# Softmax sums turned by block transposes on VectorE instead of products on TensorE, in an attention and convolution kernel

## The chip, the core and the metric

The kernel runs on one core of a Trainium2 chip. The metric is the device time of one execution in microseconds (us); the median of three runs stands for the kernel. PE is TensorE, DVE VectorE, ACT ScalarE, POOL GpSimd, and SP the engine that issues most DMAs. "PEld" is the part of PE that loads weights.

## The reference

Two independent results are put side by side: `a`, a long convolution over 2048 positions of 448 channels (an S4D state-space layer), and `b`, full softmax attention with 16 heads of width 28. The change touches `b` alone:

```python
q, k, v = qkv[0], qkv[1], qkv[2]
scale = Dh ** -0.5
scores = jnp.einsum("bhqd,bhkd->bhqk", q, k) * scale
p = _softmax(scores, axis=-1)
o = jnp.einsum("bhqk,bhkd->bhqd", p, v)
return o.transpose(0, 2, 1, 3).reshape(B, S, D) @ wo
...
return jnp.concatenate([a, b], axis=-1)
```

## The kernel before

A first phase (about 0 to 230 us) projects `q`, `k` and `v` and prepares tables for the convolution; there a scheduler orders the instructions. From then on every engine executes its instructions in the order in which the program wrote them (`nc.kept = KEPT["a"]`), each engine strictly in its own order.

The second phase is one loop of 256 steps (`for s in range(NS)`). The 16 heads are 4 groups of 4, the 2048 queries 4 stretches of 512, so there are 16 **units**, numbered 0 to 15; each has 16 steps, one for each 128 keys. A step's order is written in `ORDER`:

- `m0` to `m3` (`max_mm`) are products for a later unit's row maxima. Each takes a PSUM tile from a ring of three, `pm0`, `pm1`, `pm2` (`w_tile`). The tile of `m0` is read by ACT (`rl`), that of `m1` by DVE (an instruction that the trace calls CUSTOM_DVE_ANT_0 and the order ISA), those of `m2` and `m3` by DVE (`TENSOR_REDUCE mx<-pm`).
- `s0` to `s3` (`s_mm`) are this step's scores (`pss`), which ACT turns to `p` by an exponential.
- `pv` (`pv_step`) adds the product of the previous step's `p` with `v` to the PSUM tile `po`.
- `f` (`slot`), two of them, one ahead of `pv` and one behind it, run one waiting job each, from several queues in a fixed order of rank. A job's PSUM tile comes from the same ring of three. Jobs are parts of the convolution (`ua,w` and `ua,mt`; `e,g` and `w,ko`; later `yk,mw`, `p,mw`, `zi,wb`), the transpose `ident,m` of the maxima, and output projections (`ua,og` and `ua,on`).
- `v` (`vec`), three of them, run DVE's next part of the convolution's powers (`g`, `zg`); `k` sends POOL its parts (`e`, `eu`), products and sums of tiles in SBUF, 9 instructions for each of 56 blocks. These go on until about 985 us.

So on PE, from one `po` to the next, a step reads: job, `m2 s2 m3 s3 m0 s0 m1 s1`, job, `po`. From step 192 on (unit 12) the ring of three becomes one name with four buffers.

`fin` closes a unit, called right after its last `pv`. `po` holds 4 heads in 4 strips of 32 partitions: 28 rows of output, and in row 28 the sum of the exponentials, because the columns of `v` carry a 1 there. ACT copies `po` to `o` (128 x 512, SBUF). Then two jobs follow in slots, 2 and 4 slots later (`soon_slot(UG[1], sums)` and `soon_slot(UG[2], scale)`): `sums` multiplies `o` with the selector `sel` on PE (in 4 strips and 4 column blocks, which gives the sums with queries on partitions), DVE takes the reciprocals `r`, and ACT spreads each over 32 columns (`rb`); `scale` turns `rb` back on PE by products with the identity `ident`, and DVE multiplies `o` with that PSUM tile to `on`. For units 0 to 11 `on` goes to DRAM, for units 12 to 15 it feeds the output projections (`project`), which `scale` queues.

## Time and profile before

| | |
|---|---|
| median of 3 runs | 1278.05 us (1277.69 to 1278.42) |
| the profiled execution | 1278.83 us, of which the span from the first to the last instruction is 1277.0 us |
| granted TensorE clock | 0.982 of full speed over the span, 1.00 from 232 to 1255 us |
| busy in the span | PE 95%, ACT 76%, DVE 72%, POOL 66%, PEld 54% |

All names in the trace's rows come from the program, with buffer numbers left out; every row has line L77, that of a helper through which all instructions pass, so rows are told apart by their tiles: `po<-p,v` is a matmul that writes `po` from `p` and `v`. "x32" in a row of PE is twice the 16 matmuls of the program, because each float32 product is made in two passes that the trace shows singly. A row of the timeline has its start, its length (both in us), engine, line, operation, tiles, shapes and count; a bracket at its end is the engine's idle time just before it, and what ended that.

### The profile page before, as it was taken

How to read it: one execution, taken by the hardware profiler on the slowest of the kernel's cores; microseconds unless marked ns; L12 is line 12 of the kernel's file. 1: busy time of each engine (PE TensorE's matmuls, PEld its weight loads, DVE VectorE, ACT ScalarE, POOL GpSimd, SP SyncE). 2: the span in 40 equal slices, each digit the busy share in tenths (PEclk: the TensorE clock that was granted, in tenths of full speed). 3: DMA queues.
4: the chain of work that ended last, by engine and by line, in shares of the span. 5: the costliest groups of instructions: out<-in, count | busy, mean ns of one | idle time of the engine just before them, and what ended most of it. 6: DMA issues, size and time to landing. Idle time of an engine off the chain costs nothing.

```text
span 1277.0 us, 33251 instructions
## 1 busy us (share of the span) xinstructions
PE 1216.2 (95%) x12593; PEld 692.5 (54%) x12593; DVE 922.6 (72%) x2106; ACT 967.0 (76%) x2162; POOL 843.6 (66%) x728
## 2 busy tenths in 40 slices
PE   6788888999999999999999999999999999999998
PEld 4666764555555555555555555555555555544433
DVE  5788966877777877778778988888887645645111
ACT  5888865788888888888888888888887656656552
POOL 2666740798788888878689999989995222324321
PEclk9999898899999999999999999999999999999999
DMA  6678789436554645475533133432224533657656
GB/s 194 211 258 290 275 278 359 124 88 187 159 154 114 169 118 159 123 224 177 171 101 96 57 80 105 145 91 71 83 60 149 171 139 135 205 162 237 203 163 174
DMA packets 203528, 206.22 MB, mean 161 GB/s; under 512 B 98344, under 2 KB 162408, under 8 KB 201320
## 3 DMA queue, kind: packets, MB, share of 16 engines
q1 hardware_dynamic: 202840, 203.50, 51.8%
q8 instruction: 99, 1.62, 0.5%
q10 hardware_dynamic: 528, 0.59, 0.2%
q14 instruction: 61, 0.50, 0.1%
HBM read 121.60 MB, written 82.18 MB: 160 GB/s over the span
## 4 chain that ended last, share of the span: by engine, by line
PE 79%; DVE 9%; ACT 5%; issue 3%; POOL 2%; DMA 1%; SPq 1%; ACTq 0%; POOLq 0%; DVEq 0%
PE pm L77 44%; PE pss L77 17%; PE po L77 17%; DVE tri L77 1%; ACT tri L77 1%; DVE mx L77 1%; DVE sg L77 1%; SPq L77 1%; ACT rl L77 1%; DVE hl L77 1%; DVE px L77 1%; ACT p L77 1%; PE pt L77 1%; POOL p L77 1%; DVE g L77 1%
## 5 line engine op out<-in xcount | busy, mean ns | idle before, releaser
L77 ACT ACTIVATE p<-pss 128x512 f32<-128x512 f32 x1024 | 561.3, 611 | 111.5 <-PE pss L77 108.4
L77 PE MATMUL pss<-qhat,khat 128*128 128x512 f32 x1024 | 402.8, 399 | 1.5 <-ACT p L77 1.4
L77 DVE TENSOR_REDUCE mx<-pm 128x1 f32<-128x512 f32 x480 | 308.3, 683 | 108.9 <-PE pm L77 106.8
L77 PE MATMUL pm<-khat,qhat 128*128 128x512 f32 x749 | 326.3, 439 | 6.6 <-ACT rl L77 4.4
L77 POOL TENSOR_TENSOR e<-e,sdb 128x256 f32<-128x256 f32 x168 | 201.8, 1201 | 111.4 <-ACT e L77 62.2
L77 PE MATMUL po<-p,v 128*32 128x512 f32 x2048 | 269.1, 594 | 0.0
L77 POOL TENSOR_TENSOR e<-e,eu 128x256 f32<-128x256 f32 x168 | 248.1, 1477 | 13.2
L77 PEld LDWEIGHTS pm<-khat,qhat 128*128 128x128 f32 x749 | 141.2, 189 | 202.8 <-ACT p L77 46.9
L77 DVE CUSTOM_DVE_ANT_0 rl<-pm,rl 128x512 f32<-128x512 f32 x259 | 178.2, 688 | 73.7 <-ACT rl L77 70.8
L77 PEld LDWEIGHTS pss<-qhat,khat 128*128 128x128 f32 x1024 | 190.4, 188 | 46.1 <-issue 10.8
L77 POOL TENSOR_TENSOR eu<-e,sdb 128x256 f32<-128x256 f32 x168 | 201.9, 1202 | 0.0
L77 POOL TENSOR_TENSOR p<-pr,pr 64x448 f32<-64x448 f32 x64 | 73.1, 1142 | 161.4 <-PE pm L77 134.7
L77 ACT ACTIVATE rl<-pm 128x512 f32<-128x512 f32 x259 | 156.8, 607 | 15.4 <-PE pm L77 9.4
L77 DVE TENSOR_TENSOR g<-g,zg 128x128 f32<-128x128 f32 x392 | 161.9, 413 | 3.4
L77 PE MATMUL pm<-kdif,qhat 128*128 128x512 f32 x249 | 100.9, 405 | 6.0 <-DVE xn L77 4.1
L77 PE MATMUL pm<-xh,khat 128*128 128x512 f32 x256 | 85.0, 423 | 12.1 <-DVE hl L77 5.3
L77 DVE TENSOR_TENSOR zg<-g,zg 128x128 f32<-128x128 f32 x224 | 88.0, 393 | 5.0
L77 PEld LDWEIGHTS pm<-e,g 128*32 128x32 f32 x3584 | 57.2, 109 | 43.9 <-issue 16.2
L77 DVE TENSOR_TENSOR pr<-pm,ub 128x448 f32<-128x448 f32 x64 | 37.0, 619 | 56.4 <-PE pm L77 42.0
L77 PE MATMUL pm<-e,g 128*32 128x64 f32 x3584 | 73.0, 222 | 1.9 <-POOL e L77 1.3
L77 ACT ACTIVATE y<-pm 128x448 f32<-128x448 f32 x48 | 26.5, 553 | 58.2 <-PE pm L77 35.9
L77 ACT ACTIVATE ub<-pm 128x224 f32<-128x224 f32 (+1 forms) x96 | 38.7, 448 | 39.5 <-PE pm L77 37.4
(135 smaller groups left out, 1436.7 us busy)
## 6 DMA issues: line engine op xcount, KB each, us to landing
sdb<-sd SPq DMA_DIRECT2D x55, 336.0 KB
qhat<-q SPq DMA_DIRECT2D x64, 256.0 KB
khat<-k SPq DMA_DIRECT2D x64, 256.0 KB
sd<-sg SPq DMA_DIRECT2D x8, 1456.0 KB
k<-hl SPq DMA_DIRECT2D x16, 512.0 KB
mw<-in_mw SPq DMA_DIRECT2D x16, 512.0 KB
sd<-qhat SPq DMA_DIRECT2D x8, 896.0 KB
yu_d<-ub SPq DMA_DIRECT2D x64, 112.0 KB
```

The lines of the kernel that those rows point to most:

```text
L77: i = f(*args, **kw)
```

## The change

`sums` and `scale` leave PE. DVE turns `o` in blocks of 32 x 32 (`nc.vector.transpose`, in the order of instructions STREAM_TRANSPOSE), so that the sum of head `j` and query `32 b + i` stands on partition `32 j + i` in column 28 of block `b`; DVE takes the reciprocals of those 16 columns; ACT spreads each over the 32 columns of its block; DVE turns that back into `on`, and multiplies `o` with `on`, both now in SBUF. There are three parts, `sums`, `spread` and `scale`, and they stand in a queue of their own, `free`: they run in the next three slots after `fin` beside that slot's job, and no longer take a slot from the queues of jobs. The selector `sel`, its load in the first phase, and its constant go.

```diff
     ident = const.tile([128, 128], F32, name="ident")
     nc.sync.dma_start(ident, a["ident"])
-    sel = const.tile([128, HG], F32, name="sel")
...
         nc.sync.dma_start(kones, a["kones"])
-        nc.sync.dma_start(sel, a["sel"])
...
         on = kq_p.tile([128, CQ], F32, name="on", bufs=2)
-        rb = kq_p.tile([128, 4, HG, 32], F32, name="rb")
         og = og_u.pop(u, None)
+        t_ = {}
+        turned = lambda: kq_p.tile([128, NK, 32], F32, name="rb")
+        flat = lambda t: t.rearrange("p b e -> p (b e)")
 
         def sums():
-            pw = w_tile()
-            for t in range(4):
-                mm32(pw[:, t * HG:(t + 1) * HG], o[:, t * 128:(t + 1) * 128], sel, start=True, stop=True)
-            r = kq_p.tile([128, 4, HG], F32, name="r", bufs=2)
-            nc.vector.reciprocal(r, pw[:, :4 * HG].rearrange("p (t h) -> p t h", h=HG))
-            nc.scalar.activation(rb, r[:, :, :, None].to_broadcast([128, 4, HG, 32]), AF.Copy)
+            t = turned()
+            nc.vector.transpose(flat(t), o)
+            t_["r"] = kq_p.tile([128, NK], F32, name="r", bufs=2)
+            nc.vector.reciprocal(t_["r"], t[:, :, DH])
+
+        def spread():
+            t = turned()
+            nc.scalar.activation(t, t_["r"][:, :, None].to_broadcast([128, NK, 32]), AF.Copy)
+            nc.vector.transpose(on, flat(t))
 
         def scale():
-            pw = w_tile()
-            for t in range(4):
-                mm32(pw[:, t * 128:(t + 1) * 128], rb[:, t].rearrange("p h e -> p (h e)"), ident, True, True)
-            nc.vector.tensor_tensor(on, o, pw, ALU.mult)
+            nc.vector.tensor_tensor(on, o, on, ALU.mult)
             if g < G - 1:
                 nc.sync.dma_start(on_d[c][g], on)
...
-        soon_slot(UG[1], sums)
-        soon_slot(UG[2], scale)
+        for i, f in enumerate((sums, spread, scale)):
+            free.append((n_slot[0] + 1 + i, f))
...
     def slot(s_):
         n_slot[0] += 1
+        while free and free[0][0] <= n_slot[0]:
+            free.popleft()[1]()
         if urgent and urgent[0][0] <= n_slot[0]:
             urgent.popleft()[2]()
```

Two places of the order show what moves, both at the end of unit 7. DVE's order before; `g` and `zg` are the convolution's powers, ISA is the reader of `m1`'s tile:

```order
L77 TENSOR_TENSOR zg_10567<-g_10521,zg_10567 128x256
L77 TENSOR_REDUCE mx_10480<-pm2_10698 128x1
L77 TENSOR_REDUCE mx_10480<-pm0_10705 128x1
L77 TENSOR_TENSOR g_10521<-g_10521,zg_10567 128x16x16
L77 ISA rl_10715,mx_10480<-pm2_10721,rl_10715 128x512
L77 ISA mx_10480 128x1
L77 TENSOR_TENSOR zg_10567<-g_10521,zg_10567 128x256
L77 RECIPROCAL r_10746<-pm0_10729 128x16
L77 TENSOR_TENSOR g_10521<-g_10521,zg_10567 128x16x16
L77 TENSOR_REDUCE mx_10480<-pm2_10771 128x1
```

And DVE's order at the same place after:

```order
L77 STREAM_TRANSPOSE rb_10471<-o_10468 128x512
L77 RECIPROCAL r_10473<-rb_10471 128x16
L77 TENSOR_TENSOR zg_10348<-g_10302,zg_10348 128x256
L77 TENSOR_REDUCE mx_10261<-pm0_10482 128x1
L77 TENSOR_REDUCE mx_10261<-pm1_10489 128x1
L77 TENSOR_TENSOR g_10302<-g_10302,zg_10348 128x16x16
L77 ISA rl_10499,mx_10261<-pm0_10505,rl_10499 128x512
L77 ISA mx_10261 128x1
L77 TENSOR_TENSOR zg_10348<-g_10302,zg_10348 128x256
L77 STREAM_TRANSPOSE on_10470<-rb_10513 128x512
L77 TENSOR_TENSOR on_10470<-o_10468,on_10470 128x512
L77 TENSOR_TENSOR g_10302<-g_10302,zg_10348 128x16x16
```

Two instructions come ahead of the first pair of reduces, and two more, in place of the reciprocal, ahead of the second pair, which follows the last row; `m1` (`pm0_10505`) writes the tile that the first reduce (`pm0_10482`) has read. PE's order before, from a job in the slot ahead of the unit's last `po` to the job in the slot ahead of the next:

```order
L77 MATMUL pm_10665<-e,g 32x64 x16
L77 MATMUL po<-p,v 32x512 x4
L77 MATMUL pm_10698<-khat,qhat 128x512
L77 MATMUL pm_10705<-khat,qhat 128x512
L77 MATMUL pm_10713<-kdif_9024,qhat 128x512
L77 MATMUL pm_10721<-khat,qhat 128x512
L77 MATMUL pm_10729<-sel,o 32x4 x16
L77 MATMUL po<-p,v 32x512 x4
L77 MATMUL pm_10754<-w_111,ko 32x128 x8
```

And after (the `pss` rows between are left out in both):

```order
L77 MATMUL pm_10446<-e,g 32x64 x16
L77 MATMUL po<-p,v 32x512 x4
L77 MATMUL pm_10482<-khat,qhat 128x512
L77 MATMUL pm_10489<-khat,qhat 128x512
L77 MATMUL pm_10497<-kdif_8836,qhat 128x512
L77 MATMUL pm_10505<-khat,qhat 128x512
L77 MATMUL pm_10516<-w_110,ko 32x128 x8
L77 MATMUL po<-p,v 32x512 x4
```

The job `w,ko` moves up into the slot that `sel,o` held, and nothing stands behind the next `po`. In the first phase the scheduler also orders some instructions otherwise, by a place or a few, on all engines.

More of the change, by code (lines that the diff above doesn't have):

```diff
@@ L926, in body @@
     k_seeds(0)
-    urgent, back = collections.deque(), collections.deque()
+    urgent, free = collections.deque(), collections.deque()
     powers = {"g": collections.deque(), "e": collections.deque()}
@@ L1121, in body @@
     s = NS
-    while urgent or p_due or m_due or u_due or any(q[k] for q in (f_jobs, f_tasks, f_loaded) for k in "sf"):
+    while urgent or free or p_due or m_due or u_due or any(q[k] for q in (f_jobs, f_tasks, f_loaded) for k in "sf"):
         slot(s)
@@ L1133, in constants @@
     k["ident"] = np.eye(128)
-    sel, ones = np.zeros((128, HG)), np.zeros((128, 1))
+    ones = np.zeros((128, 1))
     for j in range(HG):
-        sel[32 * j + DH, j] = 1.0
         ones[32 * j + DH:32 * j + DH + 2] = 1.0
-    k["sel"], k["kones"] = sel, ones
+    k["kones"] = ones
     k["pw2"] = np.tile(2.0 ** np.arange(LV), (128, 1))
```

## The prediction

> **What bounds the kernel now.** First the page: busy time and the shares of the chain that ended last.

> ```profile
> PE 1216.2 (95%) x12593; PEld 692.5 (54%) x12593; DVE 922.6 (72%) x2106; ACT 967.0 (76%) x2162; POOL 843.6 (66%) x728
> PE 79%; DVE 9%; ACT 5%; issue 3%; POOL 2%; DMA 1%; SPq 1%; ACTq 0%; POOLq 0%; DVEq 0%
> ```

> PE is busy for 95% of the span and carries 79% of the chain. But a full PE says little about how much room the others have, so next comes the busy time by stage, here 700 to 800 us, in the middle of the loop.

> ```profile
> 700.00:800.00 100.00, 99.57 (x1218) 56.95 (x1218) 87.53 (x210) 84.49 (x191) 96.26 (x78) 1.00 0.28 80
> ```

> PE 99.6%, DVE 87.5%, ACT 84.5%, POOL 96.3%. PE is the bound, DVE and POOL stand right behind it. So what counts is whether DVE's new work fits at its place, not in the mean. For that I read the timeline over the end of unit 7.

> ```profile
> 733.02 1.04 PE L77 MATMUL po<-p,v 128*32 128x512 f32 x8
> 734.00 0.50 PE L77 MATMUL pm<-khat,qhat 128*128 128x512 f32 x1
> 734.16 0.60 ACT L77 ACTIVATE o<-po 128x512 f32<-128x512 f32 x1 [0.15 <-PE po L77]
> 734.27 0.43 DVE L77 TENSOR_TENSOR zg<-g,zg 128x256 f32<-128x256 f32 x1
> 734.61 1.28 DVE L77 TENSOR_REDUCE mx<-pm 128x1 f32<-128x512 f32 x2
> 735.50 0.39 PE L77 MATMUL pm<-khat,qhat 128*128 128x512 f32 x1
> 735.73 0.40 PE L77 MATMUL pss<-qhat,khat 128*128 128x512 f32 x1
> 735.81 0.41 DVE L77 TENSOR_TENSOR g<-g,zg 128x256 f32<-128x256 f32 x1
> 736.05 0.43 PE L77 MATMUL pm<-sel,o 128*32 128x4 f32 x32
> 736.33 1.06 PE L77 MATMUL po<-p,v 128*32 128x512 f32 x8
> 736.39 1.11 ACT L77 ACTIVATE p<-pss 128x512 f32<-128x512 f32 x2
> 736.55 0.69 DVE L77 CUSTOM_DVE_ANT_0 rl<-pm,rl 128x512 f32<-128x512 f32 x1 [0.33 <-PE pm L77]
> 737.76 0.50 PE L77 MATMUL pm<-khat,qhat 128*128 128x512 f32 x1
> 737.79 0.63 ACT L77 ACTIVATE rb<-r 128x512 f32<-128x512 f32 x1 [0.28 <-DVE r L77]
> 740.17 1.08 PE L77 MATMUL pm<-ident,rb 128*32 128x128 f32 x32
> 741.06 1.04 PE L77 MATMUL po<-p,v 128*32 128x512 f32 x8
> ```

> Matmuls overlap in the trace, so PE's prices are differences of starts: `m2` comes at 734.00, `m1` 1.50 us later. DVE's first reduce ends near 735.27, only 0.2 us ahead of `m1`, which needs that tile (ring of three). How hard that link is shows where an earlier product already costs DVE time, at the transpose of the maxima:

> ```profile
> 723.48 0.48 PE L77 MATMUL pm<-khat,qhat 128*128 128x512 f32 x1
> 724.07 0.28 DVE L77 SCALAR_TENSOR_TENSOR mh<-pm,mh 16x128 fp32r<-16x128 f32 x1
> 724.61 1.27 DVE L77 TENSOR_REDUCE mx<-pm 128x1 f32<-128x512 f32 x2
> 725.34 0.50 PE L77 MATMUL pm<-khat,qhat 128*128 128x512 f32 x1 [0.17 <-DVE mx L77]
> ```

> Two DVE instructions of 0.28 us push the reduces back, and `m1` starts 1.86 us after `m2` in place of 1.50: 0.36 us lost on PE. So DVE's delay there reaches PE one for one, less a margin of about 0.2.

> **What is removed.** `sel,o` holds PE from 736.05 to 736.33, 0.28 us; `ident,rb` from 740.17 to 741.06, 0.89: 1.17 together. The whole of the two groups bounds it from above:

> ```profile
> L77 PE MATMUL pm<-ident,rb 128*32 128x128 f32 x512 | 17.3, 275 | 0.6 <-ACT rb L77 0.6
> L77 PE MATMUL pm<-sel,o 128*32 128x4 f32 x512 | 7.0, 175 | 0.3 <-ACT o L77 0.3
> L77 DVE TENSOR_TENSOR on<-o,pm 128x512 f32<-128x512 f32 x16 | 10.9, 682 | 2.3 <-PE pm L77 2.1
> L77 DVE RECIPROCAL r<-pm 128x16 f32<-128x16 f32 x16 | 4.0, 251 | 0.3 <-PE pm L77 0.3
> ```

> 24.3 us over 16 units is 1.52 each. Between the two ends I take 1.35 where small waits of the old chain go too (units 0 to 11: 16.2 us) and 1.17 for units 12 to 14 (3.5 us). PE is the bound there, so this counts in full. The two freed slots don't add to it: jobs move up into them, but the sum of PE's work is what counts.

> The last unit's end is a chain of its own:

> ```profile
> 1254.40 0.60 ACT L77 ACTIVATE o<-po 128x512 f32<-128x512 f32 x1 [1.14 <-PE po L77]
> 1256.54 1.08 PE L77 MATMUL pm<-ident,rb 128*32 128x128 f32 x32 [0.63 <-ACT rb L77]
> 1257.43 2.44 PE L77 MATMUL pm<-ua,og 128*32 128x448 f32 x24
> 1259.69 0.94 PE L77 MATMUL pm<-ua,on 128*32 128x448 f32 x8
> ```

> `o` is there at 1255.00. After: turn 0.68, reciprocal 0.25, ACT 0.63, turn 0.68, product 0.68 and some 0.04 for each handover make `on` ready near 1258.1; PE does the 2.26 us of `og` meanwhile. So `on`'s product starts 1.6 us earlier. Removed in all: 16.2 + 3.5 + 1.6 = 21.3 us.

> **What is added, and where it lies.** On DVE two block turns and a product from SBUF, less the 0.68 us product from PSUM. No row shows a block turn. [...] I take 0.68, since all 512-wide rows with one result per element have that.

> ```profile
> L77 DVE TENSOR_SCALAR tri<-tri 128x1232 f32<-128x1232 f32 x8 | 8.5, 1062 | 0.0
> 92.96 1.02 POOL L77 TENSOR_TENSOR qhat<-qhat 128x336 f32<-128x336 f32 x1
> 93.18 1.17 DVE L77 TENSOR_TENSOR sg<-tri 128x336 f32<-128x336 f32 x1
> 115.00 0.50 DVE L77 TENSOR_TENSOR sg<-tri 128x336 f32<-128x336 f32 x1
> L77 POOL TENSOR_TENSOR e<-e,eu 128x1024 f32<-128x1024 f32 x56 | 133.6, 2386 | 4.4
> L77 POOL TENSOR_TENSOR e<-e,sdb 128x256 f32<-128x256 f32 x56 | 35.3, 631 | 102.6 <-ACT e L77 62.2 <-DMA sdb<-sd 39.8
> ```

> [...]

> The product has another price. A DVE product with both inputs in SBUF took 0.50 us alone, but 1.17 when a POOL product on SBUF was under way: it ended 0.37 after POOL's. The loop before has no such pair, since `zg` and `pm` lie in PSUM; the new `on<-o,on` is one, and POOL is 96% busy. A wait lies between 0 and a whole POOL instruction, which has 0.63 to 2.39 us; I take 0.6, somewhat under half of the middle between them, for POOL is not always busy and 0.1 of DVE's own start runs beside the wait. [...]

> *First step after `fin`, unit 7.* The turn waits for `o`, which ACT ends at 734.76. Behind it in DVE's queue stand the reciprocal, `zg` and the two reduces, and PE's `m1` waits for the first reduce, the next job for the second. Turn 734.80 to 735.48, reciprocal to 735.73, `zg` to 736.16, first reduce to 736.84: `m1` at 736.87 in place of 735.50. 1.37 us lost.

> *Second step.* The last scores `s1` start at 737.10, the job at 737.5, when the second reduce has ended; `po` follows 0.5 later, `m2` 0.98 behind it (as 734.00 behind 733.02) at 738.95, so `m1` is due at 740.45. ACT's second pair of `p` ends 1.77 us after the start of `s1` (735.73 to 737.50), then come a `yk` or the like and `rb`: it is there between 738.7 and 739.5. DVE has `g`, the 0.69 us reader of `m1` (ISA) and `zg` until 739.0, turns until 739.7 or a little later, waits 0.6 and multiplies until 740.96, does `g` until 741.4 and the first reduce until 742.05: `m1` at 742.1, 1.65 us lost. In the third step DVE is level again, for PE waited.

> Units differ in one thing above all, a job between `po` and `m2`, as in the two-job steps of the first half:

> ```profile
> 357.61 0.94 PE L77 MATMUL pm<-ua,w 128*32 128x448 f32 x8
> 358.47 0.50 PE L77 MATMUL pm<-khat,qhat 128*128 128x512 f32 x1
> ```

> It sets `m1` back by 0.86 us less what the handover takes, and so hides as much. By the order of the changed kernel the first step has it in units 1, 2, 3, 5 and not in eight, the second in 0, 1, 4, 5 and not in eight. The same arithmetic gives for the first step 8 x 1.35 + 4 x 0.5 = 12.8 us, and for the second, with some steps that have no job at all, 8 x 1.8 + 4 x 0.8 = 17.6: 30.4 us. Units 12 to 14 lose nothing: their ring has four buffers and DVE has no powers left. POOL waits some 0.5 us for DVE's product in each unit; PE's own loss covers it. ACT has the same two copies as before, `rb` a slot earlier or so; SP sends `on` to DRAM earlier, past one load of `sdb` or `qhat` at most, and nothing reads it before the last four units. The `sel` load and the first phase's other order, an instruction of up to 0.74 us by a few places, I put at 0, with 3 us either way.

> Sum: 30.4 - 21.3 = +9.1 us on the profiled execution, 1278.83 to 1287.9; that one lies 0.8 above the median, so the forecast is 1287 us.

> **The rivals.** *DVE has room.* By the mean it has 12% idle; if the turns slip into idle time (DVE waits 108.9 us in all for `pm`), only the removal counts: 1278 - 21.3, about 1257 us. For it: those 108.9 us. Against it: 0.2 us of margin at `m1`.

> ```profile
> L77 DVE TENSOR_REDUCE mx<-pm 128x1 f32<-128x512 f32 x480 | 308.3, 683 | 108.9 <-PE pm L77 106.8
> ```

> It decides from the point where the losses of a unit stay under 1.35 us. Chance 0.14. *Half the loss.* Turns of 0.44, no wait for POOL: 2 x 0.24 + 0.6 less for each of 12 units, 13 us less: 1274, chance 0.08. *Slow turns.* 1.36 us each: 2 x 0.68 x 12 = 16 us more: 1303, chance 0.10. That PE's products don't go isn't open: the order shows them gone. The forecast keeps 0.68.

> **How the numbers follow.** A measurement can tell 0.2%, 2.6 us. The forecast's own range is 1276 to 1299 (wait for POOL 0 to 1.2 us: 7 us either way; first phase 3; turn 0.1 off: 2.4). Reaching half into the two outer cases beside it, 1269 to 1303 leaves out the first rival and little more. Faster: 0.14 + 0.06 of the second; same 0.04; slower 0.76.

> **What would show it.** Right: in the loop, PE idle before `pm<-khat,qhat` twice a unit, 1 to 2 us, released by DVE `mx`; steps behind `fin` near 5 us without `sel,o`; `on<-o,on` longer than 0.68 in the mean up to 985 us and 0.68 after. Wrong: steps of 3.5 us there and no PE idle (first rival); STREAM_TRANSPOSE rows far from 0.68; or a first phase that ends elsewhere than near 232 us by more than 3.

## The result, and the profile after

The changed kernel takes 1313.94 us (median of 4 runs, 1311.5 to 1314.4) against 1278.18 us before: 1.0276 times as long, 95% interval 1.0259 to 1.0294. The forecast was 1287, the range ended at 1303. The sign was right, the size was not. The profiled execution took 1313.85 us, its span 1312.0.

The page of the kernel after, busy time and the shares of the chain that ended last:

```profile
PE 1210.0 (92%) x11569; PEld 675.0 (51%) x11569; DVE 952.0 (73%) x2138; ACT 968.6 (74%) x2162; POOL 846.0 (64%) x728
PE 70%; DVE 13%; ACT 7%; POOL 4%; issue 4%; DMA 1%; SPq 0%; ACTq 0%; POOLq 0%; DVEq 0%
```

PE has 6 us less busy time than before, though 24.3 us of products went, in part because some of its work ran at half clock, as will be seen. DVE, ACT and POOL stand in the chain with 24% where they had 16%.

The new instructions, as groups of the kernel after (tiles, shapes, count, busy time and mean ns, idle time ahead):

```profile
L77 DVE TENSOR_TENSOR on<-o,on 128x512 f32<-128x512 f32 x16 | 20.8, 1300 | 0.5
L77 DVE STREAM_TRANSPOSE rb<-o 128x512 f32<-128x512 f32 x16 | 11.4, 713 | 13.1 <-ACT o L77 13.1
L77 DVE STREAM_TRANSPOSE on<-rb 128x512 f32<-128x512 f32 x16 | 11.4, 710 | 5.6 <-ACT rb L77 5.1
```

A turn takes 0.71 us. The product takes 1.30 in the mean, 0.62 more than the same product from PSUM before. It is 0.69 where no POOL instruction runs beside it (unit 1) and up to 2.15 where one has just begun (unit 9).

Now the place that the prediction worked out, the end of unit 7, in the timeline after:

```profile
752.26 0.50 PE L77 MATMUL pm<-khat,qhat 128*128 128x512 f32 x1
...
753.05 0.71 DVE L77 STREAM_TRANSPOSE rb<-o 128x512 f32<-128x512 f32 x1 [0.55 <-ACT o L77]
...
754.29 1.27 DVE L77 TENSOR_REDUCE mx<-pm 128x1 f32<-128x512 f32 x2
...
755.02 0.50 PE L77 MATMUL pm<-khat,qhat 128*128 128x512 f32 x1 [1.10 <-DVE mx L77]
...
757.12 0.50 PE L77 MATMUL pm<-khat,qhat 128*128 128x512 f32 x1
...
757.64 1.30 POOL L77 TENSOR_TENSOR e<-e,eu 128x512 f32<-128x512 f32 x1
757.68 1.81 DVE L77 TENSOR_TENSOR on<-o,on 128x512 f32<-128x512 f32 x1
...
759.75 1.28 DVE L77 TENSOR_REDUCE mx<-pm 128x1 f32<-128x512 f32 x2
...
760.48 0.50 PE L77 MATMUL pm<-khat,qhat 128*128 128x512 f32 x1 [1.71 <-DVE mx L77]
...
761.68 2.01 PE L77 MATMUL po<-p,v 128*32 128x512 f32 x8
```

From `m2` to `m1` PE takes 2.76 us in the first step and 3.36 in the second, in place of 1.50: 1.26 and 1.86 lost, where 1.37 and 1.65 were forecast. The product starts 0.04 us after a POOL product and ends 0.55 us after it. The last row, already in the third step, is what the prediction had not reckoned with: the eight `po` records take 2.01 us, where they took 1.04 before.

To see where the 35 us between the two spans come from, I take the start of ACT's copy `o` at each unit's end from both traces:

```
                                before     after    difference
start to end of unit 0          293.17    300.81       +7.64
end of unit 0 to end of 11      669.42    690.05      +20.63
end of unit 11 to the end       314.44    321.17       +6.73
```

In the first line the change has not executed a single instruction of its own yet. The second is the loop with the powers; the third is one step of 10.45 us near 1008 us (3.56 before), less small gains.

**The clock.** PE's wait in unit 6's second step, and the windows of the kernel after around it (start and end, length, busy time of PE, PEld, DVE, ACT and POOL, granted clock, DMA share, GB/s):

```profile
699.87 0.63 PE L77 MATMUL pm<-khat,qhat 128*128 128x512 f32 x1 [2.62 <-DVE mx L77]
...
696.70:700.10 3.40, 0.78 (x4) 0.35 (x3) 3.37 (x5) 1.79 (x4) 3.40 (x2) 1.00 0.11 41
700.10:703.50 3.40, 3.40 (x42) 1.15 (x41) 2.28 (x6) 1.13 (x3) 3.32 (x3) 0.50 0.90 272
```

PE waits 2.62 us for `mx`, is busy for 0.78 of 3.40 us, and for the next 3.41 us has half the clock: up to 1.7 us more (an estimate, half of 3.41), after the wait is over. Four such periods begin between 240 and 985 us after, at 440.68, 700.09, 761.53 and 880.99, and none before.

**The step at 1008 us.** PE's and POOL's timelines after:

```profile
1018.04 1.08 PE L77 MATMUL pm<-e,g 128*32 128x64 f32 x32 [6.48 <-POOL e L77]
```

```profile
1006.96 4.78 POOL L77 TENSOR_TENSOR p<-pr,pr 64x448 f32<-64x448 f32 x4 [13.81 <-DVE pr L77]
1011.82 1.91 POOL L77 TENSOR_TENSOR e<-e,sdb 128x1024 f32<-128x1024 f32 x1
1013.68 1.91 POOL L77 TENSOR_TENSOR eu<-e,sdb 128x1024 f32<-128x1024 f32 x1
1015.67 2.32 POOL L77 TENSOR_TENSOR e<-e,eu 128x1024 f32<-128x1024 f32 x1
```

And POOL's before:

```profile
968.83 2.40 POOL L77 TENSOR_TENSOR e<-e,eu 128x1024 f32<-128x1024 f32 x1
980.11 4.80 POOL L77 TENSOR_TENSOR p<-pr,pr 64x448 f32<-64x448 f32 x4 [8.88 <-PE pm L77]
```

Before, the last powers of the last block stand ahead of the inverse transform's first products `p`. After, they stand behind them. The slots that `sums` and `scale` no longer take let the job `last` run in the slot ahead of `k` in its step (its products `yk,mw` stand behind `po` after, ahead of `po` before), instead of one slot later, behind `k`; so `p`, which has to wait for PE and DVE, came in front of three powers that waited for nothing, and PE's `e,g` waited 6.48 us for these.

### The profile page after: what moved, and what is told of

Same layout as the page of the kernel before. It is cut to its first block, busy times and chain, and to the rows that moved or that the text cites. A ratio compares the mean times of both kernels' runs of the same rounds, so it can differ in the third digit from the quotient of the medians.

```text
span 1312.0 us, 31222 instructions
## 1 busy us (share of the span) xinstructions
PE 1210.0 (92%) x11569; PEld 675.0 (51%) x11569; DVE 952.0 (73%) x2138; ACT 968.6 (74%) x2162; POOL 846.0 (64%) x728
## 4 chain that ended last, share of the span: by engine, by line
PE 70%; DVE 13%; ACT 7%; POOL 4%; issue 4%; DMA 1%; SPq 0%; ACTq 0%; POOLq 0%; DVEq 0%
PE pm L77 39%; PE po L77 15%; PE pss L77 14%; DVE mx L77 2%; DVE on L77 2%; ACT p L77 2%; ACT rl L77 1%; ACT tri L77 1%; DVE tri L77 1%; POOL e L77 1%; POOL p L77 1%; DVE zg L77 1%; DVE px L77 1%; DVE g L77 1%; DVE rl L77 1%
## 5 line engine op out<-in xcount | busy, mean ns | idle before, releaser
L77 ACT ACTIVATE p<-pss 128x512 f32<-128x512 f32 x1024 | 563.0, 610 | 136.6 <-PE pss L77 132.3
L77 PE MATMUL pss<-qhat,khat 128*128 128x512 f32 x1024 | 403.1, 400 | 2.0 <-ACT p L77 2.0
L77 DVE TENSOR_REDUCE mx<-pm 128x1 f32<-128x512 f32 x480 | 308.2, 683 | 105.0 <-PE pm L77 102.7
L77 PE MATMUL pm<-khat,qhat 128*128 128x512 f32 x749 | 329.5, 443 | 32.0 <-DVE mx L77 26.4
L77 POOL TENSOR_TENSOR e<-e,sdb 128x256 f32<-128x256 f32 x168 | 202.5, 1205 | 128.8 <-ACT e L77 80.5
L77 PE MATMUL po<-p,v 128*32 128x512 f32 x2048 | 273.3, 603 | 0.0
L77 PEld LDWEIGHTS pm<-khat,qhat 128*128 128x128 f32 x749 | 141.5, 189 | 254.1 <-DVE mx L77 57.1
L77 POOL TENSOR_TENSOR e<-e,eu 128x256 f32<-128x256 f32 x168 | 249.1, 1483 | 13.2
L77 DVE CUSTOM_DVE_ANT_0 rl<-pm,rl 128x512 f32<-128x512 f32 x259 | 178.1, 688 | 63.2 <-ACT rl L77 60.2
L77 PEld LDWEIGHTS pss<-qhat,khat 128*128 128x128 f32 x1024 | 191.3, 189 | 45.3 <-issue 11.0
L77 POOL TENSOR_TENSOR eu<-e,sdb 128x256 f32<-128x256 f32 x168 | 203.8, 1213 | 0.0
L77 POOL TENSOR_TENSOR p<-pr,pr 64x448 f32<-64x448 f32 x64 | 73.1, 1142 | 149.5 <-PE pm L77 107.5
L77 ACT ACTIVATE rl<-pm 128x512 f32<-128x512 f32 x259 | 156.7, 606 | 14.5 <-PE pm L77 8.0
L77 DVE TENSOR_TENSOR g<-g,zg 128x128 f32<-128x128 f32 x392 | 162.2, 414 | 3.5
L77 PE MATMUL pm<-kdif,qhat 128*128 128x512 f32 x249 | 99.8, 401 | 6.0 <-DVE xn L77 4.3
L77 PE MATMUL pm<-xh,khat 128*128 128x512 f32 x256 | 85.9, 430 | 17.0 <-DVE kb L77 8.9
L77 DVE TENSOR_TENSOR zg<-g,zg 128x128 f32<-128x128 f32 x224 | 87.9, 392 | 5.0
L77 PE MATMUL pm<-e,g 128*32 128x64 f32 x3584 | 74.5, 224 | 8.3 <-POOL e L77 8.3
L77 PEld LDWEIGHTS pm<-e,g 128*32 128x32 f32 x3584 | 56.5, 111 | 47.3 <-issue 12.9
L77 ACT ACTIVATE ub<-pm 128x224 f32<-128x224 f32 (+1 forms) x96 | 38.9, 450 | 41.7 <-PE pm L77 41.2
L77 DVE TENSOR_TENSOR pr<-pm,ub 128x448 f32<-128x448 f32 x64 | 37.0, 619 | 44.9 <-PE pm L77 25.9
L77 ACT ACTIVATE y<-pm 128x448 f32<-128x448 f32 x48 | 26.6, 554 | 57.7 <-PE pm L77 35.1
```

The costliest lines, as they stand in the source:

```text
L77: i = f(*args, **kw)
```

## The experiments

"Loop" is the time from unit 0's end to unit 11's, and all times but the median are of the profiled execution. One table, since most comparisons are between kernels of it:

```
            median   unit 0 ends   loop    unit 11 to the end
before     1278.18     293.17     669.42        314.44
after      1313.94     300.81     690.05        321.17
a_sel      1301.69     291.26     688.24        319.97
k_sel_late 1287.54     301.27     669.14        315.32
b_flush    1304.69     299.99     690.50        312.45
e_ab       1296.01     292.04     689.23        312.84
c_zg       1299.73     301.83     676.21        321.21
d_pool     1313.92     300.09     689.78        319.73
g_fill     1291.46     292.08     683.69        312.72
f_spaced   1274.48     291.13     671.37        309.18
m_135      1279.81     291.58     674.85        310.16
h_defer    1273.02     292.38     655.77        323.66
l_defer2   1274.61     292.47     655.64        324.21
i_psum     1269.65     292.40     665.83        309.09
```

**1. The first phase** (`a_sel`, `k_sel_late`). One puts the load back into the changed kernel, the other moves it in the kernel before to the start of the second phase.

```diff
+    sel = const.tile([128, HG], F32, name="sel")
...
         nc.sync.dma_start(kones, a["kones"])
+        nc.sync.dma_start(sel, a["sel"])
```

> The changed kernel with the unused load of sel kept, so that every engine's order in the first phase is that of the kernel before, up to the end of unit 0. If the order makes the first phase longer: unit 0 ends (copy o) at 293.2 us as before, in place of 300.8, and the median falls by 7.6 to about 1306. If the 7.6 us are chance of the profiled execution, or come from elsewhere: median 1312 to 1315, and unit 0 ends near 300.8.

```diff
-        nc.sync.dma_start(sel, a["sel"])
...
+    nc.sync.dma_start(sel, a["sel"])
     u_load(0)
     u_load(1)
```

> The kernel before, with the load of sel moved to the start of the second phase: the first phase then has the changed kernel's order on every engine, the rest its own. If that order is longer by itself: unit 0 ends near 301 us in place of 293, about 1287. If not: 1278.

Unit 0 ends at 291.26 us with the old order and at 301.27 with the new one in the kernel that is otherwise as before. The medians follow: 1301.69, 12.2 less than the changed kernel, and 1287.54, 9.4 more than before. The other kernels of the table fall into the same two groups by this order, 291.1 to 293.2 and 300.0 to 301.8. So some 9 us of the 35.8 are not the work of the turns: with one DMA fewer, the scheduler of the first phase put the instructions of all engines into another order, and that order is longer. The traces bear the two orders out: up to 225 us `k_sel_late` has that of the changed kernel on every engine, `a_sel` that of the kernel before. What in the new order costs the time stays open. (The other 3 us of `a_sel` lie at two places: a half clock near 430 us that did not occur, and the last product, which had POOL's `ut` in its way in the changed kernel and took 2.15 us there, 0.69 here.)

**2. POOL's order at the end of the powers** (`b_flush`; `e_ab` has both edits).

```diff
             forth(1)
+            while powers["e"]:
+                powers["e"].popleft()()
             join(0)
```

> The changed kernel, with POOL's last three powers (e, eu) of the last block issued ahead of the products p of the first inverse job. If the 10.45 us step at 1008 us comes from their order on POOL's queue: that step is near 3.5 us, no half clock behind it, median down by 7.9 to about 1306. If POOL is only late there and p then comes late: the back products wait, half is given back, about 1310. Nothing else may change before 985 us.

> The changed kernel with both earlier edits: the load of sel kept, and the last powers ahead of the products p. If the two losses are separate, their gains add: 1313.9 - 12.2 - 9.2 = 1292.5. If one of them only moves a wait that the other has too: 1296 or more.

POOL's timeline in `b_flush`, the last power and `p`:

```profile
996.71 2.69 POOL L77 TENSOR_TENSOR e<-e,eu 128x1024 f32<-128x1024 f32 x1
1007.26 4.80 POOL L77 TENSOR_TENSOR p<-pr,pr 64x448 f32<-64x448 f32 x4 [7.85 <-DVE pr L77]
```

The powers are done 8 us before `p` can start. No half clock is left near 1014 us, and the time from unit 11's end falls from 321.17 to 312.45, 8.7 us, of which 1.5 are that same last product. `e_ab` comes out at 1296.01, where the second expectation begins (1296 or more), but not for its reason: in its trace both gains are there in full (unit 0 ends at 292.04, the last stretch has 312.84), and what it lacks against 1292.5 is `a_sel`'s missing half clock and the 1.5 us that both had counted.

**3. The product's wait for POOL** (`c_zg`, `d_pool`).

```diff
-            nc.vector.tensor_tensor(on, o, on, ALU.mult)
+            if u < 12:
+                four = on.rearrange("p (c n) -> p c n", c=4)
+                nc.vector.tensor_tensor(four, four, zgs[max(zgs)][:, None, :128].to_broadcast([128, 4, 128]), ALU.mult)
+            else:
+                nc.vector.tensor_tensor(on, o, on, ALU.mult)
```

> The changed kernel, with the product of units 0 to 11 reading on (SBUF) and the PSUM tile zg in place of o and on: it leaves out the multiplication by o and keeps a DVE product of 512 with one input in SBUF. If the wait for POOL's instruction is what costs: the product takes 0.68 in each unit, no PE wait over 1.5 us and no half clock between 235 and 985 us; 12 x 0.70 of waits and 4 x 1.7 of half clock go, 15 us, about 1299. If the turns and the product as such cost it: less than 5 us gained, 1309 or more.

The group in `c_zg`:

```profile
L77 DVE TENSOR_TENSOR on<-on,zg 128x512 f32<-128x512 f32 x12 | 8.2, 687 | 0.4
```

With one input in PSUM a product of this size takes 0.69 us, with POOL busy beside it (ten of the twelve) or not. The loop is 13.8 us shorter, no half clock is left in it, and the longest wait of PE in units 0 to 10 is 1.46 us. The median, 1299.73, is the expected 1299. In the changed kernel the twelve products of units 0 to 11 waited 8.4 us together; the rest of the 13.8, 5.4 us, fits the four half clocks (5.5 by experiment 4).

```diff
-            nc.vector.tensor_tensor(on, o, on, ALU.mult)
+            (nc.gpsimd if u < 12 else nc.vector).tensor_tensor(on, o, on, ALU.mult)
```

> The changed kernel, with the product of units 0 to 11 on POOL in place of DVE. If DVE's queue is what PE waits for and POOL has room: 12 x 1.38 us leave DVE, half clocks go (4 x 1.7): 1291. If POOL, 96% busy, has no room: 12 products of 1.06 us push the powers back, e,g waits for e, up to 12 us are given back: 1303.

Worse than the worse of the two expectations: 1313.92, nothing gained. Two groups of `d_pool`:

```profile
L77 PE MATMUL pm<-e,g 128*32 128x64 f32 x3584 | 74.1, 224 | 22.8 <-POOL e L77 22.8
...
L77 POOL TENSOR_TENSOR on<-o,on 128x512 f32<-128x512 f32 x12 | 15.4, 1285 | 83.0 <-DVE on L77 83.0
```

The product leaves DVE, but on POOL it waits for DVE's turn (83.0 us of idle time) with the powers queued behind it, and PE waits 22.8 us for powers, three of them followed by a half clock (638, 826 and 942 us). That is not the expected want of room: POOL's idle time ahead of the first power of a block (`e<-e,sdb 128x256`) falls from 120.1 us in the changed kernel to 44.9, so POOL had been idle there anyway. What costs is the place: POOL keeps its order, and the powers now come after a product that has to wait for DVE.

**4. The clock itself** (`g_fill`). If a wait costs twice, once as a wait and once as a half clock, work that fills the wait should take the second away without touching the first.

```diff
-        nc.tensor.matmul(pss, kt_g[u // NQ][j][:, kt * 128:(kt + 1) * 128], q_u[u][:, j, :], start=True, stop=True)
+        for _ in range(1 + 9 * (j == 0 and kt == 2 and u - 1 in (2, 6, 7, 9))):
+            nc.tensor.matmul(pss, kt_g[u // NQ][j][:, kt * 128:(kt + 1) * 128], q_u[u][:, j, :], start=True, stop=True)
```

> As e_ab, with the first scores product s0 of the third step after fin (the one whose m1 waits 1.7 to 2.6 us) made ten times in units 2, 6, 7 and 9, always with the same result: 9 x 0.23 = 2.07 us of work in PE's wait. If the clock is halved because PE idles: the half clocks near 440, 690, 750 and 870 us are gone, and 3 to 4 times 1.7 us with them, less the 0.4 us by which the work is longer than unit 7's wait: 4 to 6 us faster than e_ab. If the clock falls for another reason: half clocks stay, and the same or slower.

PE's timeline at unit 6's second step in `g_fill`, and the window from there on:

```profile
686.40 2.50 PE L77 MATMUL pss<-qhat,khat 128*128 128x512 f32 x10
689.43 0.50 PE L77 MATMUL pm<-khat,qhat 128*128 128x512 f32 x1 [0.53 <-DVE mx L77]
```

```profile
688.80:692.20 3.40, 2.87 (x46) 1.47 (x46) 3.26 (x8) 1.73 (x4) 3.32 (x2) 1.00 0.69 158
```

`m1` still waits for `mx`; PE does nine useless products meanwhile, and the clock stays at 1.00. All four half clocks of the loop are gone and 5.5 us with them (689.23 to 683.69; median 4.6 less), 1.4 us for each: 36 products more, and faster. So the half clock is a consequence of PE's waiting.

**5. The place of the three parts** (`f_spaced`, on `e_ab`; `m_135` goes back by one slot from there).

```diff
-            free.append((n_slot[0] + 1 + i, f))
+            free.append((n_slot[0] + 2 + 2 * i, f))
```

> As e_ab, with sums, spread and scale 2, 4 and 6 slots after fin in place of 1, 2 and 3: each stands ahead of the po of another step, behind the reader of m1, where DVE has up to 0.25 us until the reduces can start. If what counts is how much DVE gets between two pairs of reduces: no PE wait over 1.5 us in units 0 to 11, no half clock, first and second step lose under 1 us each; 6 to 9 us faster than e_ab. If DVE's total is what counts: the same as e_ab within 2.

```diff
-            free.append((n_slot[0] + 2 + 2 * i, f))
+            free.append((n_slot[0] + 1 + 2 * i, f))
```

> As f_spaced, with sums, spread and scale 1, 3 and 5 slots after fin: still one in a step, but the first turn stands again in the step of fin, where DVE can begin it only when ACT has copied o, after the reduces could start. If the wait for o in front of the reduces is what costs in the first step: 1.1 to 1.4 us for each of 12 units come back, 1287 to 1291. If only the number of DVE instructions in a step counts: 1275 as f_spaced.

`f_spaced` runs 1274.48, 21.5 us faster than `e_ab` where 6 to 9 were expected, and faster than the kernel before: 0.9972 times its time, 0.9961 to 0.9983. The instructions on DVE are the same, and so are their lengths:

```profile
L77 DVE TENSOR_TENSOR on<-o,on 128x512 f32<-128x512 f32 x16 | 20.7, 1291 | 0.0
```

The product waits for POOL as before (8.3 us over units 0 to 11, 8.4 in the changed kernel). What differs is that no step has to take more than one of the three, and no wait between 235 and 985 us passes 1.5 us. My expectation had counted the half clocks (5.5 us) and little else; but DVE stands idle in every step, 0.67 us in the mean of the loop before (117.5 us in 176 steps), and three steps have more of that than one.

How much, the traces show step by step. The table has the length of each step behind `fin`, from the start of one `po` to that of the next, less the same step of `h_defer` (experiment 6), where DVE has no new work; in us, summed over units 0 to 10:

```
             step 1   step 2   step 3   step 4
after          11.5     17.6      5.5      0.1
c_zg           11.5      9.4     -0.2      0.0
g_fill         11.7     16.2     -0.2      0.0
f_spaced        0.0      4.9      3.1      7.7
m_135          11.6      3.4      4.0     -0.1
i_psum          0.1      6.3      2.1      1.9
```

The first turn costs 11.6 us in the step of `fin`, 1.06 a unit, where DVE can begin it only when `o` is there, and 4.9 a step later. That `m_135` still loses only 3.5 us of loop against `f_spaced` (0.32 a unit; the median, 1279.81, lies 1.0015 times the kernel before, 1.0005 to 1.0024) has another cause: its product, in step 3, waits 3.3 us for POOL over the twelve units, that of `f_spaced`, in step 4, 8.3. Two places changed at once: the turn's costs 6.7 us more, the product's 3.7 less.

**6. The work moved to another time** (`h_defer`, `l_defer2`). For units 0 to 11 `fin` stores `o` as it is; `load_og` then queues the three parts for each loaded tile.

```diff
     def load_og(u):
         og_u[u] = og = kq_p.tile([128, G - 1, CQ], F32, name="og")
         nc.sync.dma_start(og, on_d[u % NQ][:G - 1].rearrange("g p q -> p g q"))
+        for g2 in range(G - 1):
+            norm(og[:, g2], og[:, g2], 4 + 3 * g2)
...
+        if g < G - 1:
+            free.append((n_slot[0] + 1, lambda: nc.sync.dma_start(on_d[c][g], o)))
+        else:
+            norm(o, on, 1, on, queue)
...
-        if kt == 12 and u // NQ == G - 1:
+        if kt == 9 and u // NQ == G - 1:
```

> As e_ab, but for units 0 to 11 o goes to DRAM as it is, with its sums in row 28, and is turned, spread and multiplied only after it is loaded again, in steps 9 to 16 of units 12 to 15, where DVE is busy for half of the time and POOL for a third; that load comes at step 9 in place of 12. If the place is what costs: units 1 to 11 run 12 to 16 us faster than in the kernel before (PE's products are gone and DVE has nothing in their place), and 12 x 2.35 us on DVE cost PE under 5 us later: 1260 to 1266. If PE waits for DVE there too: 1275 or more.

```diff
+        d = 1 if u == NU - 1 else 2
...
-            norm(og[:, g2], og[:, g2], 4 + 3 * g2)
+            norm(og[:, g2], og[:, g2], 3 + 3 * d * g2, d)
...
-        if kt == 9 and u // NQ == G - 1:
+        if kt == 8 and u // NQ == G - 1:
...
-        f_loaded[kind].append((max(f_ready.get((kind, f), 0), s_ + FL[kind]), tasks))
+        f_loaded[kind].append((max(f_ready.get((kind, f), 0), s_ + FL[kind] + ((kind, f, i) == ("s", 0, 0))), tasks))
```

> As h_defer, with the first inverse job a step later (in h_defer it waits 2.3 us for its load yk, and a half clock follows), and the nine parts for units 0 to 11 two slots apart from step 9 on, except in the last unit. If those waits made the 14 us that units 12 to 15 lose there: half of them come back, about 1266. If DVE's added work does: 1272.

The loop is where PE's products are gone and DVE has nothing in their place: 655.77 us, 13.65 less than before, 1.24 a unit. That is the measured worth of the removal, with the old product and reciprocals on DVE and ACT's copy `rb` gone from the loop as well. The other half failed: the last stretch takes 323.66 us, 9.2 more than before, and 10.8 more than in `e_ab`, which keeps units 12 to 15 as the change has them. So two thirds of the 13.65 are paid back there. `l_defer2` was to show that two waits did that; the half clock near 957 us went, as expected, but the total did not (1274.61): the stretch behind unit 11 is 5.2 us shorter, that behind unit 14 4.3 longer. (Each of the two has one later half clock as well, near 1172 and 1230 us.) This points to DVE's added work in units 12 to 15, or where it stands in them; which of the two stays open.

**7. A version without the wait for POOL** (`i_psum`, on `f_spaced`). The reciprocals lie in PSUM, in the free columns of `zg`'s bank; the turned `o` is multiplied by them in its turned form, and the second turn gives `on`. ACT's copy is no longer needed.

```diff
-            t_["r"] = kq_p.tile([128, NK], F32, name="r", bufs=2)
+            t_["r"] = (zg_one[:, Z_G + 256 + NK * (u % 2):Z_G + 256 + NK * (u % 2) + NK] if u < 11 else kq_p.tile([128, NK], F32, name="r", bufs=2))
...
-            t = turned()
-            nc.scalar.activation(t, t_["r"][:, :, None].to_broadcast([128, NK, 32]), AF.Copy)
-            nc.vector.transpose(on, flat(t))
+            t = t_["t"]
+            nc.vector.tensor_tensor(t, t, t_["r"][:, :, None].to_broadcast([128, NK, 32]), ALU.mult)
...
-            nc.vector.tensor_tensor(on, o, on, ALU.mult)
+            nc.vector.transpose(on, flat(t_["t"]))
```

> As f_spaced, but the reciprocals of units 0 to 10 lie in the free columns of zg's bank in PSUM, the turned o is multiplied by them (one input in SBUF), and the second turn makes on from that: no DVE product with both inputs in SBUF is left, and ACT's copy rb goes. In f_spaced the twelve products were 8.3 us longer than 0.68 each. If these waits reach PE: the product takes 0.68, and 4 to 6 us go, about 1269. If the spacing hides them already: 1274 as f_spaced.

Its groups, eleven units with the reciprocals in PSUM and five with them in SBUF:

```profile
L77 DVE TENSOR_TENSOR rb<-rb,zg 128x512 f32<-128x512 f32 x11 | 7.5, 682 | 0.1
L77 DVE TENSOR_TENSOR rb<-rb,r 128x512 f32<-128x512 f32 x5 | 6.9, 1373 | 0.0
```

0.68 us against 1.37 for the same product. 1269.65 us: 5 us less than `f_spaced`, and 0.9937 times the kernel before (0.9920 to 0.9953). It beats both. Two things go at once, the wait for POOL and ACT's copy between the turns, and no run parts them; by the table of experiment 5 most of the gain, 5.8 us, lies in step 4, where `f_spaced` has its product.

## Why the prediction was wrong

It is easiest to see on the profiled execution, +9.1 forecast against +35.0 (the spans).

- *The turn, the wait for POOL, the places.* Right. 0.68 us forecast for a turn, 0.71 measured; 0.6 for the wait, 0.70 in the mean of units 0 to 11; the losses at `m1` of unit 7 within about 0.2 us. The second of these is in part luck: the wait in unit 7 was 1.13 us, but the turn ahead of it started 0.2 earlier than forecast. From unit to unit the wait lies between 0 and 1.47. The traces bear the wait out: products of 0.69 with one input in PSUM (`c_zg`), of 0.67 to 2.15 with both in SBUF (`after`). The turns of two rivals, 0.44 (an estimate: the 1.06 us of TENSOR_SCALAR `tri<-tri`, scaled from 1232 columns to 512) and 1.36 (twice 0.68), no run shows: all 32 turns of the changed kernel took 0.70 to 0.72.
- *What the removal is worth.* 1.35 a unit forecast, 1.24 measured (`h_defer`); over the loop's 11 units 1.2 us too much.
- *What is added.* The step that failed is "in the third step DVE is level again, for PE waited". Without unit 11, the forecast's 30.4 us are 27.3 for the loop's 11 units: 11.5 in the first step, 15.8 in the second, nothing in the third. Measured are 690.05 - 655.77 = 34.3, by steps 11.5, 17.6 and 5.5 (the table of experiment 5; later steps give 0.3 back). The first step is right; of the 1.8 more in the second a part is the half clock of unit 6, which begins in that step. The 5.5 of the third lie wholly in units 2, 6, 7 and 9, with 0.9 to 1.6 us each; in the other seven units the third step does lose nothing. These four are the units with a half clock, and where it doesn't occur (`c_zg`, `g_fill`) the third step loses nothing either. The price of a wait was taken as its length; where it left PE busy for half of a stretch of 3.41 us or less (0.34, 0.23, 0.50 and 0.30 in units 2, 6, 7 and 9) it was some 1.4 us more (5.5 over four in `g_fill`). The forecast's own second step, 1.65 us, stood just short of that point, and those with a longer wait for POOL went over it. (The sum put 1.8 for that step and gave no reason for more than 1.65.)
- *The first phase.* "I put at 0, with 3 us either way": measured 7.6 in this execution, 9.4 by the medians of `k_sel_late`. The order had been read as moved by a place or a few; in the traces up to 225 us some 230 of PE's 740 instructions stand elsewhere, 41 of them by more than ten places, and I had no row that would have priced it. The range should have held it. The prediction's own sign, a first phase that ends elsewhere by more than 3 us, came true.
- *"Units 12 to 14 lose nothing."* One step at unit 12's start lost 6.9 us, 7.9 with the half clock behind it. Two jobs moved up were costed at nothing, since the sum of PE's work is what counts; but a job is also DVE's and POOL's instructions, and on POOL it passed three powers. That could be read from POOL's order beforehand.
- *The end.* 1.6 us forecast, 1.2 measured, 2.8 in `a_sel`, where the last product had no POOL product to wait for. The products of units 12 to 14 gave 1.6 in place of 3.5.

The sum: forecast 9.1, + 7.6 first phase, + 8.2 in the loop (7.0 and 1.2), + 7.9 at 1008 us, + 2.2 of smaller gains behind it that did not come: 35.0. None of the rivals had these; "slow turns" had the size of the added work for a cause that wasn't there.

What failed of the range is that all its terms were sizes of the mechanism that I knew. Two of the three large misses lie outside of it, in places where none of the change's instructions stands.

## What to carry to other kernels

On balance with the products that PE saves, the same DVE instructions cost this loop 20 us or 2, by the slots they stood in: where an engine waits for another by a margin of tenths, spread new work one instruction to a step, and place it where the other engine's idle time is, not behind the event that makes its input. Read the order of every engine that a moved job touches, not only of the engine whose work went. And a wait on PE had a second price here, some 1.4 us, where it left PE busy for 0.23 to 0.50 of a stretch of 3.41 us (units 2, 6, 7 and 9).

## What was not expected of the hardware

*The clock window.* The half clocks come in periods of 3.41 us or multiples, at a fixed raster in each execution: in the kernel after they last 3.41, 6.83 or 10.24 us, but for the one at the very end, and from one start to another lie whole multiples of 3.41 (76 from 440.68 to 700.09 us). I cut the 14 profiled executions of these kernels, from 235 us on and without the last 10 us of each, along that raster, and took PE's busy share in each window at full clock:

```
busy share of a window       windows    followed by a half clock
0.39 and less                   20                20
0.44 to 0.50                     8                 5
0.51 to 0.70                    75                 0
```

*POOL waits for DVE too.* The rows below are from the timeline of `i_psum`. The product of unit 11 with both inputs in SBUF starts 0.58 us after a POOL product and takes 2.32 us; in unit 13 the two start within 0.01 us of each other, DVE's takes its 0.69, and POOL's takes 2.68, 0.58 more than the 2.10 that the same one has at 1248.05. With `r` in PSUM, 64 bytes a partition, eleven such products take 0.68 each with POOL busy beside them.

```profile
964.51 2.35 POOL L77 TENSOR_TENSOR e<-e,eu 128x1024 f32<-128x1024 f32 x1
965.09 2.32 DVE L77 TENSOR_TENSOR rb<-rb,r 128x512 f32<-128x512 f32 x1
...
1107.91 0.69 DVE L77 TENSOR_TENSOR rb<-rb,r 128x512 f32<-128x512 f32 x1
1107.91 2.68 POOL L77 TENSOR_TENSOR ut<-ut,dsk 128x896 f32<-128x896 f32 x1 [4.42 <-DMA dsk<-in_A_D_skip]
...
1248.05 2.10 POOL L77 TENSOR_TENSOR ut<-ut,dsk 128x896 f32<-128x896 f32 x1 [5.13 <-DVE ot L77]
```
